# One table for the small weights, a later place for a split chunk's second value copies and for the zero block

## The chip, the cores and the metric

The kernel runs on one core of a Trainium2 chip. The metric is the time of one execution in device microseconds (us). Engines are named as the profile names them: PE is TensorE's matmuls and PEld its weight loads, DVE is VectorE, ACT is ScalarE, POOL is GpSimd, SP is SyncE, which here only issues transfers (DMAs).

## The reference

Three stages follow each other. Linear attention on q, k, v of shape (4, 8, 576, 64); an expert layer that sends each of the 2304 tokens to one of 8 experts (at most 576 tokens each); and a dense layer with a gate `h - tanh(h)`.

```
def phi(x):
    proj = np.einsum('bhsd,df->bhsf', x, w_phi)          # w_phi: 64 x 128
    proj = proj - np.max(np.abs(proj), axis=-1, keepdims=True)
    return np.concatenate([np.exp(proj), np.exp(-proj)], axis=-1)
q_p, k_p = (phi(q), phi(k))
kv = np.einsum('bhsf,bhsd->bhfd', k_p, v);  z = np.sum(k_p, axis=2)
out = einsum(q_p, kv) / (einsum(q_p, z) + 1e-06)
...
logits = x @ w_gate                                      # w_gate: 512 x 8
expert_idx = np.argmax(logits, axis=1)                   # then relu(x @ w1) @ w2 of that expert
...
h = x @ w_in;  out = (h - np.tanh(h)) @ w_out
```

## The kernel before

The 2304 tokens are 18 chunks of 128 rows. The attention is a loop over steps s = 0, 1, ... (line 761). Step s projects the keys of chunk s (`proj`, line 311, PE), subtracts the row maxima (`sub`, lines 319 and 322, DVE), takes both exponentials (`kexp`, lines 333 and 334, ACT), and sums keys times values of the chunk before into PSUM (`kv_step`, line 359, PE). From step 5 on (`LAG = 5`) the same step also projects the queries of chunk s - 5, transposes and exponentiates them (line 397), forms the numerator (`num`, line 458) and stores the rows (`xs`, line 536). Beside this a conversion works through the dense layer's weights, one piece a step: four transfers bring a piece (line 119, `raw`), and lines 93 (ACT), 98 to 106 (DVE, POOL), 282 (ACT) and 285 (POOL) turn it into two fp32r halves.

The expert logits are linear in v, so `vgate` (line 343, PE) multiplies each chunk's values by `w_gate` and ACT copies the result, and a column of ones, into the value tile beside the values (lines 347 and 350), before `kv_step` uses it. In steps 0 to 4 `vgate` stands ahead of the step's exponentials, from step 5 on behind them. Chunks 4 and 13 lie across two batches. They have two value tiles, one for each batch, with 64 rows each; `kv_step` uses the first and `kv_second` the second, after the first batch's sums are copied out (line 369).

Two small weights are needed at once: `wphi` (w_phi twice, one copy in each half of the partitions), for line 311, and `wgb` (w_gate laid out as blocks between zeros), for line 343. They come by four transfers on ACT's queue (lines 207 and 209); `wgb` is set to zero by DVE first. All other loads go out on SP's queue in the order of the program. Each transfer of the SP and ACT queues takes the next of eight semaphores in turn, so an issue waits until the transfer that had the same semaphore has landed; it also waits for its buffer. Keys, queries and transposed values have two buffers each, `raw` has two pieces, value tiles are three. The tile `d` between lines 322 and 333 has one buffer for the keys, and so has the result `kp` of lines 333 and 334 in most steps.

A block of zeros, `zs` (128 x 512 f32), is written to DRAM in step 7 (line 854). It is read much later, when the output is cleared (line 1179).

Nothing plans the order: each engine runs its instructions as the program issues them, and waits only on semaphores.

Of the kernel before, what the change touches and what calls it, by code (L numbers as in the profile page):

```python
# [8 lines left out]
F32 = mybir.dt.float32  # L9
# [7 lines left out]
P = 128  # L17
B, H, S, D = 4, 8, 576, 64
NT = B * S
DM = H * D  # L20
DF = 128
E = 8
FF = 1024
FF2 = 2048
NCH = NT // P
# [9 lines left out]
S2, T2 = -2.33084472, 2.44485132  # L35


def build(nc, tc, ctx, qT, kT, vT, v, w_phi, w_gate, w12, win, wout, out, cap):
    capn = min(cap, NT)
    G = max(1, -(-capn // UNIT))  # L40
    SL = G * UNIT
# [31 lines left out]
    sb = psp.tile([P, 512], F32, name="sb")  # L73
# [68 lines left out]
    def attention():  # L142
        st, stq = ExitStack(), ExitStack()
        LAG = 5
        ca = st.enter_context(tc.tile_pool(name="ca", bufs=1))
# [13 lines left out]
        HB = D + 1 + E  # L159
# [3 lines left out]
        GP = 2 * E  # L163
        PRE, CNT = 64, 512 - E

        wphi = ca.tile([P, DF], F32, name="wphi")
        wgb = ca.tile([P, 4, GP], F32, name="wgb")
        tri = ca.tile([P, P], BF16, name="tri")
        ones = ca.tile([P, P], BF16, name="ones")
        e16 = ca.tile([P, E], F32, name="e16")  # L170
# [4 lines left out]
        cum = ca.tile([P, E], BF16, name="cum")  # L175
        zero = ca.tile([P, P], F32, name="zero")

        nc.vector.memset(wgb, 0.0)
        nc.vector.memset(zero, 0.0)
        nc.vector.memset(ones, 1.0)  # L180
        nc.vector.memset(sq_b[:, 0:1], S1)
# [3 lines left out]
            out=tri, in_=ones, compare_op=ALU.is_gt, fill=0.0, base=0,  # L185
# [17 lines left out]
        nc.gpsimd.iota(tokv[:, :, 1], pattern=[[0, NCH]], base=0, channel_multiplier=1,  # L203
                       allow_small_or_imprecise_dtypes=True)

        for j in range(2):
            nc.scalar.dma_start(out=wphi[64 * j:64 * j + 64], in_=w_phi)
        for j in range(2):
            nc.scalar.dma_start(out=wgb[64 * j:64 * j + 64, :, j * E:(j + 1) * E],
                                in_=w_gate[:, 64 * j:64 * j + 64].rearrange("c p e -> p c e"))  # L210

        kin, qin, vtin = {}, {}, {}
        NV = 3
# [1 line left out]
        strad = {4: (0, 1), 13: (2, 3)}  # L215

        vuse, vslot, nv, done = {}, {}, 0, {}
# [12 lines left out]
        def ldk(c):  # L230
            t = ink.tile([P, DM], F32, tag="k", name="k")
            nc.sync.dma_start(out=t, in_=kT[c])
            kin[c] = t
# [44 lines left out]
        def cv_main(i):  # L278
            yield from cv_bits(raw.pop(i), cva.pop(i), cvm.pop(i))

        def cv_hi(i):
            nc.scalar.copy(pieces[i][1], cvw[i])
# [24 lines left out]
        def proj(kind, i, ps):  # L307
            src = (kin if kind == "k" else qin)[i]
            for hp in range(4):
                for g in range(2):  # L310
                    nc.tensor.matmul(ps[:, g, hp * DF:(hp + 1) * DF],  # L311
                                     src[64 * g:64 * g + 64, hp * P:(hp + 1) * P], wphi[64 * g:64 * g + 64],
                                     start=(hp == 0), stop=(hp == 3), skip_group_check=True)
            psk[kind, i] = ps.rearrange("p g (a b) -> p (g a) b", b=DF)
# [12 lines left out]
        def kexp(i):  # L327
            t = kd.pop(("k", i))
            if i in (1, 3):
                e = qp_p.tile([P, 2, H, P], F32, tag="qp", name="qp").rearrange("p s h f -> p h s f")  # L330
            else:
                e = kp_p.tile([P, H, 2, DF], F32, tag="kp", name="kp")
            nc.scalar.activation(out=e[:, :, 0, :], in_=t, func=AF.Exp)
            nc.scalar.activation(out=e[:, :, 1, :], in_=t, func=AF.Exp, scale=-1.0)
            kp[i] = e

        def vgate(c):
            vg = sb[:, 0:4 * GP].rearrange("p (a b) -> p a b", b=GP)
            ps = vg[:, :, 0:2 * E].rearrange("p a (b e) -> p a b e", e=E)
            for hp in range(4):  # L340
                for a in range(2):
                    o = hp * P + 64 * a
                    nc.tensor.matmul(vg[64 * a:64 * a + 64, hp, :], vtin[c][:, o:o + 64], wgb[:, hp],
                                     start=(hp == 0), stop=(hp == 3), skip_group_check=True)
            for a, t in enumerate(vuse[c]):
                lo, hi = (64 * a, 64 * a + 64) if c in strad else (0, P)
                nc.scalar.copy(t[lo:hi, :, D:D + 1], ones[lo:hi, 0:H].unsqueeze(2))
            for a, t in enumerate(vuse[c]):
                lo, hi = (64 * a, 64 * a + 64) if c in strad else (0, P)
                nc.scalar.copy(t[lo:hi, :, D + 1:HB].rearrange("p (a b) e -> p a b e", b=2), ps[lo:hi])  # L350

        def kv(i, vt, first, last):
            for g in range(2):
# [407 lines left out]
        for s in range(LAST + 1):  # L761
            i, j, jt = s, s - LAG, s - LAG - 1
            jn = jt if s < SD else jt - 1 if s > SD else -1
            kk, qq, tt = i < NCH, 0 <= j < NCH, 0 <= jt < NCH
            pc, pd = CV.get(s), CV.get(s - 1)
            since = {cs: s - (cs[-1] + LAG + 1) for cs in subs}
            if s == SK:
                stk.close()
                mo["alloc"]()
                qpools.append(stq.enter_context(tc.tile_pool(name="qp2", bufs=1)))  # L770
                mo["spare"](qpools[-1])
                mo["rows"](zero)
            if kk:
                proj("k", i, xb if i > LAG or i % 2 == 0 else yb)
            if s >= LAG:
                cv_load(s + 2 - LAG, 0, 1)
            if s + 2 < NCH:
                ldk(s + 2)
            if s >= LAG:
                cv_load(s + 2 - LAG, 2)  # L780
            if kk:
                if i < LAG:
                    vgate(i)
            if tt:
                trans(jt)
                qexp(jt, 0)
                qexp(jt, 1)
            if since[subs[-1]] == 3:
                prefix(early)
            if 0 <= i - 1 < NCH - 1:  # L790
                kv_step(i - 1)
            if kk:
                for _ in sub("k", i):
                    pass
            bits = iter(()) if pc is None else cv_main(pc)
            run(itertools.islice(bits, 2))
            if qq:
                proj("q", j, xb)
            if 0 <= j + 2 < NCH:
                ldq(j + 2)  # L800
            if s >= LAG:
                cv_load(s + 2 - LAG, 3)
            else:
                for k in ((), (0, 1), (2, 3), (4, 5), (6, 7))[s]:
                    cv_load(k // 4, k % 4)
            if i - 1 in strad:
                kv_second(i - 1)
            if i == NCH:
                kv_step(i - 1)
                first_ids()  # L810
            if pd is not None:
                cv_hi(pd)
                cv_lo(pd)
            if kk:
                kexp(i)
            wgen = iter(())
            if since[subs[-1]] == 3:
                wgen = itertools.chain(route2(early), table(early))
                run(itertools.islice(wgen, 5))
            if qq:  # L820
                for _ in sub("q", j):
                    pass
            smalls = []
            for cs in subs:
                d = since[cs]
                if d == 1:
                    rgen[cs] = route1(early, cs[0], cs[-1] + 1)
                if 1 <= d <= 3 and cs in rgen:
                    cut = (5,) if cs == subs[-1] else (2, 5)
                    smalls.append(itertools.islice(rgen[cs], *cut[d - 1:d]) if d <= len(cut) else rgen[cs])  # L830
            smalls.append(wgen)
            if s == NCH:
                smalls.append(fgen["t"])
            if s == SK:
                smalls.append(fgen["u"])
            weave([], smalls)
            flush()
            for _ in bits:
                pass
            if 0 <= jn < NCH:  # L840
                num(jn)
            if LAG <= i < NCH:
                vgate(i)
            if CV.get(s + 1) is not None:
                cv_mag(CV[s + 1])
            if s == SK:
                mo["first"]()
            if s + 2 < NCH:
                ldvt(s + 2)
            for c, a in vslot.get(s, []):  # L850
                if c > 1:
                    ldv(c, a)
            if s == 7:
                nc.sync.dma_start(out=zs.rearrange("t (a b) -> t a b", a=4),
                                  in_=zero.unsqueeze(1).to_broadcast([P, 4, P]))
            if 0 <= jn < NCH:
                xstore([jn])
            while rstore:
                rstore.pop()()
            if s >= SK:  # L860
                mo["drain"](s - SK)
            if s == SK + 3:
                rgen["a"] = route1(tailg, 0, NA)
                run(itertools.islice(rgen["a"], 5))
            if s == SK + 4:
                run(rgen["a"])
# [559 lines left out]
```

## Time and profile before

| what | us |
|---|---|
| median of three runs | 674.19 (674.09 to 676.39) |
| the profiled execution | 675.93 |
| its span, first to last instruction | 674.2 |
| PE busy | 642.6 (95%) |
| DVE busy | 522.3 (77%) |
| ACT busy | 411.9 (61%) |

The span is from the first to the last instruction; 1.7 us of the execution lie outside. The attention steps fill about the first 180 us. PE's share of busy time covers stages with different limits, and a matmul counts as busy for longer when the granted clock is low, so each stage is read by itself. In the windows the columns are busy time of each engine with its number of instructions, then the granted TensorE clock as a share of full speed (1.00 is 2.4 GHz, 0.50 is 1.2 GHz), the mean busy share of the 16 DMA engines, and GB/s. A row of the timeline gives start, busy time, engine, line, operation, tiles and count, and in brackets how long the engine was idle before it and what released it. A row marked SPq or ACTq is the issue of a transfer, not its landing.

### The profile page before, as it was taken

To read this page: it belongs to the slowest core of one execution; us is meant where nothing else is said; L and a number is where in the kernel's file an instruction comes from. 1 tells how busy PE (TensorE), PEld (TensorE's weight loads), DVE (VectorE), ACT (ScalarE), POOL (GpSimd) and SP (SyncE) were. 2 spreads that over 40 slices of the span, in tenths; PEclk is the share of its full clock that TensorE was granted. 3 is DMA by queue.
4 is the path that set the end of the run, shared out by engine and by line. 5 is a ranking of instruction groups with operands and counts; after the bars stand their busy time and mean duration, and the time that the engine had idled before them with its cause. 6 is when DMAs were issued, how large, how long until landed. Compare 5 with 4: busy or idle time off the path is not lost. (4 is left out here: it accounts for less than half of the span.)

```text
span 674.2 us, 17422 instructions
## 1 busy us (share of the span) xinstructions
PE 642.6 (95%) x7107; PEld 626.3 (93%) x7107; DVE 522.3 (77%) x773; ACT 411.9 (61%) x720; POOL 241.4 (36%) x182
## 2 busy tenths in 40 slices
PE   8799899998999999999999999999999999999993
PEld 7798888887999999999999999999999999999992
DVE  3789799997877879989876648888976547888982
ACT  3567887776744576677554536668645527658661
POOL 1255555554200234524530104633460102553361
PEclk7999899999999999999999999999999999999998
DMA  7969788725455634222225500101214530100221
GB/s 222 321 210 298 249 278 272 245 72 182 131 166 186 189 112 150 86 68 80 74 60 166 182 17 32 37 1 40 80 48 152 168 107 1 41 13 1 87 70 40
DMA packets 45481, 83.12 MB, mean 123 GB/s; under 512 B 7840, under 2 KB 8480, under 8 KB 45392
## 3 DMA queue, kind: packets, MB, share of 16 engines
q1 hardware_dynamic: 39664, 68.99, 32.4%
q0 software_dynamic: 2624, 8.13, 4.2%
q10 hardware_dynamic: 3104, 4.80, 2.1%
q8 instruction: 58, 0.95, 0.6%
q14 instruction: 31, 0.25, 0.1%
HBM read 73.31 MB, written 13.31 MB: 128 GB/s over the span
## 5 line engine op out<-in xcount | busy, mean ns | idle before, releaser
L1029 POOL TENSOR_SCALAR al<-ut 128x576 fp32r<-128x576 f32 (+1 forms) x51 | 84.1, 1649 | 152.2 <-ACT ut L1025 82.8
L924 DVE TENSOR_TENSOR w<-raw,w 128x512 fp32r<-128x512 f32 x102 | 71.1, 712 | 44.2 <-ACT w L919 43.6
L919 ACT CAST w<-raw 128x512 fp32r<-128x512 f32 x102 | 61.9, 620 | 60.2 <-DMA raw<-w 30.0
L937 PE MATMUL xb<-xh,w_in_h 128*128 128x288 f32 x264 | 79.5, 301 | 1.1 <-ACT ut L1025 1.1
L939 PE MATMUL xb<-xh,w_in_l 128*128 128x288 f32 x264 | 78.3, 297 | 0.0
L938 PE MATMUL xb<-xl,w_in_h 128*128 128x288 f32 x264 | 78.2, 296 | 0.0
L1076 POOL DMA_INDIRECT out<-row,ids x18 | 20.3, 1126 | 114.7 <-DVE row L1074 76.6
L1016 DVE TENSOR_TENSOR al<-y,ah 128x576 fp32r<-128x576 f32 (+1 forms) x51 | 40.4, 792 | 24.6 <-ACT ah L1015 24.6
L1024 ACT COPY hs<-xb 128x576 f32<-128x576 f32 (+1 forms) x36 | 21.6, 599 | 59.1 <-DVE th L1047 30.3
L319 DVE TENSOR_REDUCE m<-xb 128x8 f32<-128x1024 f32 x33 | 40.3, 1221 | 18.1 <-PE xb L311 17.9
L938 PE MATMUL kvb<-al,w_oa_h 128*128 128x288 f32 x180 | 53.4, 297 | 0.3 <-DVE al L1016 0.3
L939 PE MATMUL kvb<-ah,w_oa_l 128*128 128x288 f32 x180 | 53.3, 296 | 0.0
L937 PE MATMUL kvb<-ah,w_oa_h 128*128 128x288 f32 x180 | 53.2, 295 | 0.0
L1040 DVE SCALAR_TENSOR_TENSOR y<-y,ut 128x576 f32<-128x576 f32 (+1 forms) x51 | 41.3, 811 | 13.4 <-ACT y L1028 13.4
L937 PEld LDWEIGHTS xb<-xh,w_in_h 128*128 128x128 f32 x264 | 49.8, 189 | 1.3 <-ACT ut L1025 1.3
L1043 DVE SCALAR_TENSOR_TENSOR y<-y,y 128x576 f32<-128x576 f32 (+1 forms) x51 | 44.9, 879 | 7.4 <-ACT y L1030 5.6
L938 PEld LDWEIGHTS xb<-xl,w_in_h 128*128 128x128 f32 x264 | 49.7, 188 | 0.0
L939 PEld LDWEIGHTS xb<-xh,w_in_l 128*128 128x128 f32 x264 | 49.6, 188 | 0.0
L359 PE MATMUL kvb<-v,kp 128*64 128x74 f32 x1152 | 43.9, 237 | 4.0 <-issue 3.3
L359 PEld LDWEIGHTS kvb<-v,kp 128*64 128x64 f32 x1152 | 40.9, 144 | 6.8 <-issue 5.5
L1048 DVE COPY_PREDICATED y<-al,th 128x576 f32<-128x576 int32 (+1 forms) x51 | 42.8, 839 | 5.6 <-DVE th L1047 0.5
L1030 ACT ACTIVATE y<-ut,sq_b 128x576 f32<-128x576 f32 (+1 forms) x51 | 38.1, 748 | 13.3 <-DVE al L1016 11.2
(292 smaller groups left out, 2148.5 us busy)
## 6 DMA issues: line engine op xcount, KB each, us to landing
raw<-w SPq DMA_DIRECT2D x105, 256.0 KB
raw<-win SPq DMA_DIRECT2D x32, 256.0 KB
raw<-wout SPq DMA_DIRECT2D x20, 256.0 KB
v<-v SPq DMA_DIRECT2D x16, 296.0 KB
k<-kT SPq DMA_DIRECT2D x18, 256.0 KB
vt<-vT SPq DMA_DIRECT2D x18, 256.0 KB
q<-qT SPq DMA_DIRECT2D x18, 256.0 KB
xs<-x SPq DMA_DIRECT2D x18, 256.0 KB
```

The lines of the kernel that those rows point to most:

```text
L319: nc.vector.tensor_reduce(out=m, in_=ps, axis=AX.X, op=ALU.max, apply_absolute_value=True)
L359: nc.tensor.matmul(kvb[bank][64 * a:64 * a + 64, col * NKV:col * NKV + VS], kp[i][:, 4 * g + hp, s, 64 * a:64 * a + 64], vt[:, 2 * hp + g, :],
L919: nc.scalar.copy(d[:, 0], t)
L924: eng.tensor_tensor(out=d[:, 1], in0=t, in1=d[:, 0].bitcast(F32), op=ALU.subtract)
L937: nc.tensor.matmul(o, ah, bh, start=first, stop=False, skip_group_check=True)
L938: nc.tensor.matmul(o, ah, bl, start=False, stop=False, skip_group_check=True)
L939: nc.tensor.matmul(o, al, bh, start=False, stop=last, skip_group_check=True)
L1016: nc.vector.tensor_tensor(out=AL[a][:, i], in0=y2[:, i], in1=AH[a][:, i].bitcast(F32), op=ALU.subtract)
L1029: nc.gpsimd.tensor_scalar(out=AL[a][:, i], in0=ut[:, i], scalar1=C2, scalar2=None, op0=ALU.is_gt)
L1040: nc.vector.scalar_tensor_tensor(out=y1[:, i], in0=y1[:, i], scalar=T1, in1=ut[:, i], op0=ALU.add, op1=ALU.mult)
L1043: nc.vector.scalar_tensor_tensor(out=y2[:, i], in0=y2[:, i], scalar=T2, in1=y1[:, i], op0=ALU.add, op1=ALU.mult)
L1048: nc.vector.copy_predicated(y2[:, i], AL[a][:, i].bitcast(I32), th[:, i])
```

## The change

The host packs w_phi (twice) and the laid-out w_gate, zeros and all, into one table of 128 x 192 f32; one transfer brings it into one tile `small`, of which `wphi` and `wgb` are slices. The DVE memset of `wgb` goes. The value copies move into a function `vcopy(c, a)`. For chunk 4 the copies of the second value tile stand behind the step's exponentials; for chunk 13 they stay where they were, with the two pairs in another order. The first two pieces of `raw` are fetched on another schedule: two transfers in each of steps 0, 1, 2 and one in each of steps 3 and 4, instead of two in each of steps 1 to 4. The zero block goes out in step 18 instead of step 7.

```
-        for j in range(2):
-            nc.scalar.dma_start(out=wphi[64 * j:64 * j + 64], in_=w_phi)
-        for j in range(2):
-            nc.scalar.dma_start(out=wgb[64 * j:64 * j + 64, :, j * E:(j + 1) * E],
-                                in_=w_gate[:, 64 * j:64 * j + 64].rearrange("c p e -> p c e"))
+        nc.scalar.dma_start(out=small, in_=w_small)
...
-        nc.vector.memset(wgb, 0.0)
...
+        def vcopy(c, a):
+            vg = sb[:, 0:4 * GP].rearrange("p (a b) -> p a b", b=GP)
+            ps = vg[:, :, 0:2 * E].rearrange("p a (b e) -> p a b e", e=E)
+            t = vuse[c][a]
+            lo, hi = (64 * a, 64 * a + 64) if c in strad else (0, P)
+            nc.scalar.copy(t[lo:hi, :, D:D + 1], ones[lo:hi, 0:H].unsqueeze(2))
+            nc.scalar.copy(t[lo:hi, :, D + 1:HB].rearrange("p (a b) e -> p a b e", b=2), ps[lo:hi])
...
+            vcopy(c, 0)
+            if c >= LAG and c in strad:
+                vcopy(c, 1)
...
-                for k in ((), (0, 1), (2, 3), (4, 5), (6, 7))[s]:
+                for k in ((0, 1), (2, 3), (4, 5), (6,), (7,))[s]:
                     cv_load(k // 4, k % 4)
...
             if kk:
                 kexp(i)
+                if i < LAG and i in strad:
+                    vcopy(i, 1)
...
-            if s == 7:
+            if s == NCH:
                 nc.sync.dma_start(out=zs.rearrange("t (a b) -> t a b", a=4),
                                   in_=zero.unsqueeze(1).to_broadcast([P, 4, P]))
```

ACT at the start of the program, before: the four weight transfers, the table of the activation function, and the first value tile's column of ones and logits.

```order
L207 DMA wphi<-w_phi 64x128 x2
L209 DMA wgb<-w_gate 64x4x8 x2
L729 ACT_TABLE_LOAD
L729 ACTIVATE few<-few 128x8
L347 CAST v_156<-ones 128x8
L350 COPY v_156<-sb 128x8x8
```

The same place in the changed kernel:

```order
L205 DMA small<-w_small 128x192
L728 ACT_TABLE_LOAD
L728 ACTIVATE few<-few 128x8
L337 CAST v_151<-ones 128x8
L338 COPY v_151<-sb 128x8x8
```

Three issues are gone from ACT's queue, and the line numbers of the rest are lower by a few.

ACT around step 4, before. `v_157` and `v_158` are the first and the second value tile of chunk 4; `kp` is the exponentials, and the last row is the conversion of the next piece.

```order
L93 ACTIVATE a<-raw 128x1024
L347 CAST v_157<-ones 64x8
L347 CAST v_158<-ones 64x8
L350 COPY v_157<-sb 64x8x8
L350 COPY v_158<-sb 64x8x8
L333 ACTIVATE kp<-d 128x8x128
L334 ACTIVATE kp<-d 128x8x128
L93 ACTIVATE a<-raw 128x1024
```

The same place in the changed kernel, where the two tiles are `v_152` and `v_153`:

```order
L93 ACTIVATE a<-raw 128x1024
L337 CAST v_152<-ones 64x8
L338 COPY v_152<-sb 64x8x8
L328 ACTIVATE kp<-d 128x8x128
L329 ACTIVATE kp<-d 128x8x128
L337 CAST v_153<-ones 64x8
L338 COPY v_153<-sb 64x8x8
L93 ACTIVATE a<-raw 128x1024
```

The two copies into the second tile have moved from ahead of the exponentials to behind them, ahead of the conversion.

SP's queue from the end of step 0 to the middle of step 2, before (k: keys, vt: transposed values, v: value tile).

```order
L232 DMA k<-kT 128x512
L237 DMA vt<-vT 128x512
L246 DMA v_158<-v 128x592
L232 DMA k<-kT 128x512
L119 DMA raw<-win 128x512 x2
L237 DMA vt<-vT 128x512
L246 DMA v_156<-v 128x592
L232 DMA k<-kT 128x512
L119 DMA raw<-win 128x512 x2
L237 DMA vt<-vT 128x512
```

The same place in the changed kernel:

```order
L227 DMA k<-kT 128x512
L119 DMA raw<-win 128x512 x2
L232 DMA vt<-vT 128x512
L241 DMA v_153<-v 128x592
L227 DMA k<-kT 128x512
L119 DMA raw<-win 128x512 x2
L232 DMA vt<-vT 128x512
L241 DMA v_151<-v 128x592
L227 DMA k<-kT 128x512
L119 DMA raw<-win 128x512 x2
```

Two `raw` transfers have moved into step 0, behind the keys of chunk 2 and ahead of the transposed values and the value tile of that chunk. The zero block stands in SP's queue between two query loads of the last attention steps instead of between a value tile and a row store. On PE and POOL the sequence is the same in both kernels.

## Rows read from the trace of the kernel before

**Rows 1.** The page, busy time and share of each engine.

```profile
PE 642.6 (95%) x7107; PEld 626.3 (93%) x7107; DVE 522.3 (77%) x773; ACT 411.9 (61%) x720; POOL 241.4 (36%) x182
```

**Rows 2.** Windows: busy (x count) of PE, PEld, DVE, ACT, POOL; clock, DMA, GB/s.

```profile
0.00:10.00 10.00, 6.92 (x59) 5.56 (x61) 3.10 (x8) 2.78 (x5) 1.72 (x15) 0.86 0.67 203
10.00:20.00 10.00, 10.00 (x206) 9.37 (x204) 4.95 (x5) 4.99 (x10) 0.58 (x1) 0.79 0.83 253
20.00:30.00 10.00, 7.65 (x192) 7.02 (x190) 8.14 (x8) 4.77 (x10) 1.29 (x2) 1.00 0.99 316
30.00:40.00 10.00, 8.43 (x176) 7.98 (x176) 6.11 (x7) 6.67 (x10) 4.01 (x2) 0.83 0.61 212
140.00:160.00 20.00, 17.79 (x379) 16.36 (x379) 18.45 (x39) 13.72 (x22) 8.86 (x6) 1.00 0.27 74
```

**Rows 3.** One window of one microsecond, shortly ahead of step 6.

```profile
35.00:36.00 1.00, 1.00 (x24) 0.92 (x21) 0.00 (x0) 1.00 (x3) 0.00 (x0) 1.00 0.02 6
```

**Rows 4.** Timeline of steps 0 and 1.

```profile
0.81 1.24 ACTq L207 DMA_DIRECT2D wphi<-w_phi  x2
...
2.08 1.32 ACTq L209 DMA_DIRECT2D wgb<-w_gate  x2
...
4.22 0.48 PE L311 MATMUL xb<-wphi,k 64*128 64x128 f32 x2
...
5.42 1.16 PE L311 MATMUL xb<-wphi,k 64*128 64x128 f32 x14 [0.71 <-DMA wphi<-w_phi]
...
7.34 0.20 ACT L347 CAST v<-ones 128x8 f32<-128x8 bf16 x1 [2.39 <-DMA v<-v]
...
7.75 1.04 PE L343 MATMUL sb<-wgb,vt 128*64 128x16 f32 x16 [1.18 <-DMA wgb<-w_gate]
...
8.72 2.08 PE L311 MATMUL yb<-wphi,k 64*128 64x128 f32 x16
...
9.13 1.06 ACT L333 ACTIVATE kp<-d 128x1024 f32<-128x1024 f32 x1
...
11.60 3.45 PE L359 MATMUL kvb<-v,kp 128*64 128x74 f32 x64
```

**Rows 5.** Timeline of steps 4 and 5, up to the first row of step 6.

```profile
23.27 0.47 SPq L246 DMA_DIRECT2D v<-v  x1
...
25.45 1.23 DVE L322 TENSOR_TENSOR d<-xb,m 128x1024 f32<-128x1024 f32 x1
...
29.05 1.22 DVE L319 TENSOR_REDUCE m<-yb 128x8 f32<-128x1024 f32 x1
...
29.33 0.20 ACT L347 CAST v<-ones 64x8 f32<-64x8 bf16 x1 [3.63 <-DMA v<-v]
...
30.03 1.06 ACT L333 ACTIVATE kp<-d 128x1024 f32<-128x1024 f32 x1
...
32.06 1.23 DVE L322 TENSOR_TENSOR d<-yb,m 128x1024 f32<-128x1024 f32 x1 [1.79 <-ACT kp L334]
...
32.08 3.33 PE L359 MATMUL kvb<-v,kp 128*64 128x74 f32 x60 [0.39 <-ACT kp L334]
33.20 0.68 DVE L98 TENSOR_SCALAR m<-raw 128x1024 int32<-128x1024 int32 x1
...
36.43 2.27 PE L359 MATMUL kvb<-v,kp 128*64 128x74 f32 x64
...
38.76 1.06 ACT L333 ACTIVATE kp<-d 128x1024 f32<-128x1024 f32 x1 [1.94 <-PE kvb L359]
...
39.09 1.16 PE L311 MATMUL xb<-wphi,k 64*128 64x128 f32 x16
```

**Rows 6.** Timeline of steps 7 to 9.

```profile
58.19 0.60 SPq L854 DMA_DIRECT2D zs<-zero  x1
...
68.68 1.17 ACT L93 ACTIVATE a<-raw 128x1024 f32<-128x1024 f32 x1 [3.71 <-DMA raw<-win]
...
71.73 3.88 PE L458 MATMUL yb<-kvs,qp 128*64 128x74 f32 x64 [1.90 <-ACT qp L397]
```

More of the change, by code (lines that the diff above doesn't have):

```diff
@@ L35, with build @@
 S2, T2 = -2.33084472, 2.44485132
-def build(nc, tc, ctx, qT, kT, vT, v, w_phi, w_gate, w12, win, wout, out, cap):
+def build(nc, tc, ctx, qT, kT, vT, v, w_small, w12, win, wout, out, cap):
     capn = min(cap, NT)
@@ L164, in attention @@
         PRE, CNT = 64, 512 - E
-        wphi = ca.tile([P, DF], F32, name="wphi")
-        wgb = ca.tile([P, 4, GP], F32, name="wgb")
+        small = ca.tile([P, DF + 4 * GP], F32, name="small")
+        wphi, wgb = small[:, 0:DF], small[:, DF:].rearrange("p (c e) -> p c e", c=4)
         tri = ca.tile([P, P], BF16, name="tri")
@@ L335, in kexp @@
             kp[i] = e
+        def vcopy(c, a):
[5 more added lines that the diff above has]
+            nc.scalar.copy(t[lo:hi, :, D + 1:HB].rearrange("p (a b) e -> p a b e", b=2), ps[lo:hi])
         def vgate(c):
             vg = sb[:, 0:4 * GP].rearrange("p (a b) -> p a b", b=GP)
-            ps = vg[:, :, 0:2 * E].rearrange("p a (b e) -> p a b e", e=E)
             for hp in range(4):
@@ L344, in vgate @@
                                      start=(hp == 0), stop=(hp == 3), skip_group_check=True)
[L345 to L350, printed above, removed]
+            vcopy(c, 0)
+            if c >= LAG and c in strad:
+                vcopy(c, 1)
         def kv(i, vt, first, last):
@@ L1395, in rows_of_v, with small_weights @@
         return r.reshape(NCH, P, H * 74)
+    def small_weights(phi, gate):
+        r = np.zeros((2, D, 2 * D + 8 * E), np.float32)
+        r[:, :, 0:2 * D] = np.asarray(phi)
+        g = r[:, :, 2 * D:].reshape(2, D, 4, 2, E)
+        for a in range(2):
+            g[a, :, :, a] = np.asarray(gate).reshape(4, 2, D, E)[:, a].transpose(1, 0, 2)
+        r[:, :, 2 * D:] = g.reshape(2, D, 8 * E)
+        return r.reshape(2 * D, -1)
     def bits(a, kt):
@@ L1408 @@
         "v": rows_of_v(inputs["v"]),
-        "w_phi": np.ascontiguousarray(inputs["w_phi"]),
-        "w_gate": np.ascontiguousarray(inputs["moe_w_gate"]).reshape(4, P, E),
+        "w_small": small_weights(inputs["w_phi"], inputs["moe_w_gate"]),
         "w12": np.ascontiguousarray(np.concatenate([w1, w2], axis=-1)),
```

## The prediction

> **What bounds the kernel now.** I read the page first: over the whole span PE is busy for 95% [rows 1]. That is a mean over stages. The windows of the first 40 us show the stage that the change touches: there PE is busy for less, part of the time at 0.83 to 0.86 of its clock, and the DMA share goes from 0.67 to 0.99 and back to 0.61 [rows 2]. So neither PE nor the transfers are full all the time; something holds both up in turn. The timeline of the same stretch shows what. In step 0 it is the small weights. The first two matmuls run at 4.22, the other fourteen wait until 5.42 for the second piece of `wphi`, and the gate product waits 1.18 more for `wgb`, until 7.75. Then step 1's projection takes 2.08 and the first sum of keys and values 3.45 [rows 4], where the same work takes 1.16 and 2.27 at full clock [rows 5]. In step 4 it is a value tile. The subtraction is done at 26.68 (25.45 + 1.23), and ACT could take the exponentials then. But it stands at the copy into the second tile of chunk 4, whose load went out at 23.27, until 29.33, and takes them at 30.03 [rows 5]. By 35 the DMA engines are idle [rows 3]. After that the steps repeat, each released by the one before, and in step 8 a conversion waits 3.71 for its piece [rows 6]. Nothing in the stages behind is tied to a clock time, so what is won by the start of step 6 is a shift of all the rest, unless a later wait eats it.
>
> **Part A, one table.** Four issues become one, the DVE memset goes, and ACT is idle there anyway, so only the landing counts. The table is 98 KB, one piece of `wphi` 33 KB. The first piece, issued at 0.81, was there at 4.22, the second at 5.42. I take 4.4 for the table: 4.22 and the 65 KB that it has more, at the 316 GB/s of the full window [rows 2], 0.2. The projection then runs from 4.4 to 5.6 instead of ending at 6.58, 1.0 earlier. The gate product follows without its wait, and step 1's projection starts near 6.6 instead of 8.72. The first exponentials go from 9.13 to 8.1 (their value tile is there at 7.34) and end at 10.1. The sum behind them starts at 10.2 instead of 11.60 and ends at 12.5 at full clock or 13.7 at half clock, instead of 15.05. That is 2.6 or 1.4. PE again stands for some 2 us ahead of it, as it did ahead of the slow rows, so I take 1.4. With a table that lands at 5.42 only 0.4 is left.
>
> Below that there is one more case. The value tile, issued on SP's queue in the same first microseconds, landed at 7.34 [rows 4]. A table that comes in no earlier than that would start the first projection 1.9 later; the gate's wait would still go, and step 1's projection would start near 9.4 instead of 8.72, so A would be -0.7. The Trainium skill has a rule on this side, in DMA: Bandwidth & Descriptors, section Issuing engines are not separate DMA queues: whoever issues them, transfers run on the same 16 DMA engines and mix. By it the table shares them with 1.1 MB of SP's loads; by the row of 4.22 a small piece came through 3.1 us ahead of the last of these. The sum would be 3.8 by the late end and 5.9 by mine.
>
> Two `raw` transfers now go out in step 0, ahead of chunk 2's transposed values and value tile. They are 0.52 MB, 1.7 us at 316 GB/s. What hides them is the idle share of the first window (0.67 busy) and the slow steps 1 and 2. If that cover is gone, they cost up to 1.7. I take nothing.
>
> **Part B, the second copies.** Without the wait ACT takes the exponentials of step 4 from 26.7 to 28.7 (they take 2.0, 30.03 to 32.06). DVE is the next to be late: the three conversion operations and the reduction that stand behind the subtraction end at 30.27 (29.05 + 1.22), so the subtraction of step 5 moves from 32.06 only to 30.3, 1.8. PE starts the sum at 28.7, needs 2.27, and with the query projection (1.16) is at 32.1. DVE is busy with its subtraction until 31.5 and with two conversion operations of 0.7 until 32.9, and then reduces and subtracts the queries (1.23 each) until 35.4. Step 6's projection waited for just that at 39.09, so it is 3.7 earlier. If PE falls to half clock in this shorter pause, the sum takes 3.5 (3.33 for 60 of the 64) and the projection 1.2 to 2.1, and the gain is 3.2 to 2.3. PE's pause is about 1 us instead of 3.5, so I take 3.4.
>
> The copies now stand behind the exponentials, ahead of the next conversion and of the copying out of the sums. The load took 6.1 from its issue at 23.27 to 29.33; with one `raw` of 0.8 less ahead of it, it lands near 28.5, just when ACT comes to it at 28.7. Issue and exponentials move together by A. The copying out needs PE's sum, at 31.0, so 2.3 of delay cost little. Chunk 13's other order costs nothing: its copies wait for no transfer. If the tile held the exponentials' followers as long as before, B would be 0.
>
> **Part C, the zero block.** Its issue took 0.60 and it moved 0.26 MB, 0.8 at 316 GB/s, at 58.19. The conversion that waits 3.71 at 68.68 has its four transfers behind it on the same queue. So the wait shrinks by 0.8 to 1.4, unless the queue drains between, then by 0. PE's sum behind this wait ran 3.88 instead of some 2.3 [rows 6]; should a shorter wait spare that, another 1.6 comes, 3.0 in all. I take 1.1. In its new place it stands between query loads where the DMA share is 0.27 [rows 2], so it costs nothing, at most its 1.4.
>
> **The sum.** 1.4 + 3.4 + 1.1 = 5.9. The profiled execution took 675.93 (span 674.2), which would become 670.0. It lies 1.74 above the median of the runs, 674.19, so the median becomes 668.3.
>
> **Rivals.** First, the transfers are the bound and the gain is given back. Up to 40 us they moved 10 us x (203 + 253 + 316 + 212) GB/s = 9.84 MB. At 316 from 2 us on, that is done at 33.1, ahead of the 34.3 at which I have step 6 start (39.09 - 4.8). But if the first 20 us stay at their mean of 228, 4.56 MB are moved by 20 and the rest takes until 36.7. Then step 6 gains only 2.4, and C nothing since the queue is never empty: 671.8. For it speaks the share of 0.99 in the third window; against it, the idle engines at 35 and that the table lets loads go out earlier. The Trainium skill, DMA: Bandwidth & Descriptors, section Specifications, gives about 358 GB/s as a core's share of the memory; an estimate with that figure is 29.5 for the 9.84 MB, and no window of 10 us here reaches it.
>
> Second, the change does only part of what it says: the table lands at 5.42 and PE stays at half clock in both places. Then A is 0.4, B 2.3 and C 0: 671.5. For it speaks that the second piece did land at 5.42 and that PE still pauses; against it, that it was issued 0.6 after the first.
>
> Third, slower: the two `raw` transfers of step 0 make chunk 2's loads late, and PE waits for transfers in steps 2 to 4. The price is the 1.7 and the half clock that follows a pause: 1.2 for a sum (3.45 against 2.27) and 0.9 for a projection (2.08 against 1.16), 2.1 a step, 6.3 for three. Those 8.0 against B and C (4.5) give 677.7. It decides from the point where the transposed values of chunk 2 land later than its projection ends, near 14. Against it: they were loaded in SP's order after 8.8 before, and the matmuls of steps 1 and 4 show no wait for a load [rows 4, 5].
>
> **How the numbers follow.** My forecast has 0.73, the transfers 0.10, the half effect 0.11, the slower case 0.06. A measurement of this kernel can tell 0.5%, 3.4 us, from no change, so the borders are 670.8 and 677.6. The forecast lies below 670.8 in nearly all of its span: its best end is 2.6 + 3.7 + 3.0 = 9.3, or 664.9; the late table, to which I give 0.08 of the 0.73, gives 674.19 - 3.8 = 670.4. The two middle rivals are within 0.5%. So faster 0.73, the same 0.21, slower 0.06. The range goes from 664.0, a little past the best end, to 672.5, past both middle rivals, since 0.27 of the chance lies beyond 670.8.
>
> **What would show it.** In the changed profile: the first projection runs its 16 matmuls in one go before 5; no gate wait; the exponentials of step 4 start within 0.3 of the subtraction's end; the copies into the second tile come behind them; step 6's projection starts at 33 to 36; the wait in step 8 is under 3. I am wrong if step 6 starts after 37, if the projection starts after 5.4, or if step 6 is early but the attention ends as late as before, since then waits for `raw` took the gain back.

## The result and the profile after

The changed kernel took 669.08 us (median of 16 runs, 665.93 to 673.46), the kernel before 674.86 in the same comparison (16 runs, 671.17 to 679.13). The medians are 5.8 apart, the means 6.3. The ratio, which goes with the means, is 0.9907 (95% interval 0.9885 to 0.9930): 6.3 us faster. A second comparison (`again`, below) gave 0.9904, interval 0.9877 to 0.9932. The profiled execution after has a span of 668.3.

The page's row of busy times after:

```profile
PE 637.6 (95%) x7107; PEld 620.9 (93%) x7107; DVE 524.1 (78%) x772; ACT 411.4 (62%) x720; POOL 240.5 (36%) x182
```

The windows of the first 40 us after, with the columns of [rows 2]:

```profile
0.00:10.00 10.00, 7.35 (x83) 5.57 (x83) 4.15 (x8) 3.36 (x6) 1.69 (x15) 1.00 0.81 260
10.00:20.00 10.00, 8.74 (x220) 8.25 (x222) 4.99 (x5) 5.30 (x11) 0.58 (x1) 1.00 0.95 307
20.00:30.00 10.00, 9.57 (x228) 8.77 (x226) 8.37 (x8) 6.79 (x10) 2.94 (x2) 1.00 0.96 295
30.00:40.00 10.00, 9.05 (x206) 8.23 (x206) 9.84 (x10) 9.06 (x14) 5.30 (x3) 1.00 0.84 270
```

The clock is 1.00 throughout, against 0.86, 0.79, 1.00 and 0.83 [rows 2], and the DMA share has no hole.

The timeline of steps 0 and 1 after, which answers to [rows 4]:

```profile
0.81 0.41 ACTq L205 DMA_DIRECT2D small<-w_small  x1
...
4.43 1.45 PE L306 MATMUL xb<-small,k 64*128 64x128 f32 x16
...
5.81 0.65 PE L345 MATMUL sb<-small,vt 128*64 128x16 f32 x16
...
6.39 1.16 PE L306 MATMUL yb<-small,k 64*128 64x128 f32 x16
6.59 0.20 ACT L337 CAST v<-ones 128x8 f32<-128x8 bf16 x1 [3.84 <-DMA v<-v]
...
10.50 2.15 PE L358 MATMUL kvb<-v,kp 128*64 128x74 f32 x60 [0.60 <-ACT kp L329]
...
12.58 1.16 PE L306 MATMUL xb<-small,k 64*128 64x128 f32 x16
```

The reader is to see that the first projection runs its 16 matmuls in one piece at 4.43, that the gate product waits for nothing, that step 1's projection comes 2.3 earlier, and that the first sum takes 2.15 for 60 matmuls where it took 3.45 for 64.

The four transfers before cost one more wait, which the rows ahead of the prediction do not show. In the list of waits of SP's queue before (total, times, longest), the issue of the transposed values of chunk 1 stands until a piece of `wphi` has landed; it is the ninth transfer, and the semaphores go round by eight:

```profile
SPq L237 <- DMA wphi<-w_phi: 1.2, 1, 1.2
```

That issue is at 3.99 before and at 2.66 after, where the list has no such wait.

The timeline of steps 4 and 5 after, which answers to [rows 5]:

```profile
21.28 0.47 SPq L241 DMA_DIRECT2D v<-v  x1
...
23.76 1.23 DVE L317 TENSOR_TENSOR d<-xb,m 128x1024 f32<-128x1024 f32 x1
...
25.02 1.06 ACT L328 ACTIVATE kp<-d 128x1024 f32<-128x1024 f32 x1 [0.58 <-DVE d L317]
...
27.05 0.20 ACT L337 CAST v<-ones 64x8 f32<-64x8 bf16 x1
...
27.07 2.15 PE L358 MATMUL kvb<-v,kp 128*64 128x74 f32 x60 [0.34 <-ACT kp L329]
...
27.36 1.22 DVE L314 TENSOR_REDUCE m<-yb 128x8 f32<-128x1024 f32 x1
...
28.69 1.23 DVE L317 TENSOR_TENSOR d<-yb,m 128x1024 f32<-128x1024 f32 x1
...
28.91 1.17 ACT L93 ACTIVATE a<-raw 128x1024 f32<-128x1024 f32 x1 [1.43 <-DMA raw<-win]
...
33.04 1.06 ACT L328 ACTIVATE kp<-d 128x1024 f32<-128x1024 f32 x1 [0.73 <-PE kvb L358]
...
33.74 1.16 PE L306 MATMUL xb<-small,k 64*128 64x128 f32 x16 [0.32 <-DVE d L317]
```

The first `L328` stands right behind the subtraction (23.76 + 1.23 = 24.99). The copy at 27.05 comes behind the exponentials and waits for nothing. The last row is the first of step 6, 5.4 earlier than before.

To see where the gain came and went, the table gives the start of a step's key projection (the first of 16 matmuls), read from the timelines. Later steps have their own waits.

| kernel | step 2 | 5 | 6 | 8 | 10 | 13 | 17 | span |
|---|---|---|---|---|---|---|---|---|
| before | 14.98 | 26.67 | 39.09 | 56.27 | 75.99 | 101.89 | 138.39 | 674.2 |
| after | 12.58 | 25.30 | 33.74 | 50.51 | 67.19 | 94.16 | 131.84 | 668.3 |
| gain | 2.4 | 1.4 | 5.4 | 5.8 | 8.8 | 7.7 | 6.6 | 5.9 |

So 1.4 are won by step 5, 4.0 between 5 and 6, 3.0 between 8 and 10, and 2.2 of it are lost again by 17.

At step 2 the gain was 2.4, and 1.0 of it is gone by step 3. Before, the sum of keys and values in step 2 ran in one piece:

```profile
16.56 2.25 PE L359 MATMUL kvb<-v,qp 128*64 128x74 f32 x64
```

After, it stops behind 45 of its 64 matmuls, for nothing that the profile shows ("issue"), and ends 3.28 after its start:

```profile
14.16 1.67 PE L358 MATMUL kvb<-v,qp 128*64 128x74 f32 x45
...
16.58 0.86 PE L358 MATMUL kvb<-v,qp 128*64 128x74 f32 x19 [0.76 <-issue]
```

The same stop is in `again` (0.54) and `u_copy` (1.03). What PE stands for there is open.

Three rows after tell of the last two stretches: the conversion in step 8 waits 2.22 instead of 3.71 [rows 6], the sum behind it takes 2.31 instead of 3.88, and a conversion in step 12 waits 3.89 (the steps of conversions are counted as in the prediction, by the step that issues them). The timeline and the issue of the zero block after:

```profile
61.43 1.22 ACT L93 ACTIVATE a<-raw 128x1024 f32<-128x1024 f32 x1 [2.22 <-DMA raw<-win]
...
64.52 2.31 PE L457 MATMUL yb<-kvs,qp 128*64 128x74 f32 x64 [0.45 <-ACT qp L396]
...
98.26 1.16 ACT L93 ACTIVATE a<-raw 128x1024 f32<-128x1024 f32 x1 [3.89 <-DMA raw<-wout]
...
143.84 0.60 SPq L855 DMA_DIRECT2D zs<-zero  x1
```

### The profile page after: what moved, and what is told of

It is laid out like the page before. It is cut to its first block, busy times and chain, and to the rows that moved or that the text cites. A ratio compares the mean times of both kernels' runs of the same rounds, so it can differ in the third digit from the quotient of the medians.

```text
span 668.3 us, 17411 instructions
## 1 busy us (share of the span) xinstructions
PE 637.6 (95%) x7107; PEld 620.9 (93%) x7107; DVE 524.1 (78%) x772; ACT 411.4 (62%) x720; POOL 240.5 (36%) x182
## 5 line engine op out<-in xcount | busy, mean ns | idle before, releaser
L938 PE MATMUL yb<-xh,w 128*128 128x288 f32 x144 | 43.8, 304 | 0.7 <-DVE al L985 0.7
L938 PE MATMUL kvb<-ah,w 128*128 128x288 f32 x144 | 42.6, 296 | 1.8 <-ACT ah L984 1.0
```

The costliest lines, as they stand in the source:

```text
L938: nc.tensor.matmul(o, ah, bh, start=first, stop=False, skip_group_check=True)
```

## The experiments

Each ratio is of the kernel's runs to runs of the kernel before on the same chip. The measured points of all of them (the columns of steps 5, 6 and 17 are the starts of their key projections, "8 to 10" is the time between two such starts):

| kernel | ratio (95%) | step 5 | step 6 | 8 to 10 | step 17 | span |
|---|---|---|---|---|---|---|
| u_copy | 0.9946 (0.9920 to 0.9972) | 26.02 | 34.55 | 17.2 | 131.87 | 667.5 |
| u_zs | 0.9915 (0.9883 to 0.9948) | 27.57 | 36.35 | 17.5 | 133.78 | 666.5 |
| u_raw | 0.9926 (0.9901 to 0.9951) | 26.12 | 35.03 | 16.8 | 132.53 | 664.3 |
| u_table | 0.9925 (0.9898 to 0.9952) | 27.93 | 36.70 | 16.7 | 132.78 | 666.4 |
| o_copy | 0.9958 (0.9931 to 0.9986) | 26.92 | 36.63 | 17.2 | 133.81 | 668.5 |
| o_table | 0.9952 (0.9925 to 0.9978) | 25.39 | 37.23 | 16.9 | 134.44 | 666.5 |
| o_raw | 0.9996 (0.9969 to 1.0023) | 27.87 | 39.90 | 18.3 | 137.59 | 675.1 |
| o_zs | 1.0002 (0.9974 to 1.0030) | 26.99 | 39.48 | 17.0 | 138.03 | 671.8 |
| again | 0.9904 (0.9877 to 0.9932) | 25.48 | 33.84 | 16.3 | 131.14 | 664.2 |
| two | 0.9914 (0.9883 to 0.9945) | 26.04 | 36.11 | 20.2 | 135.11 | 669.1 |
| b_part3 | 0.9861 (0.9835 to 0.9888) | 25.58 | 34.34 | 16.2 | 129.93 | 662.9 |
| o_part3 | 0.9975 (0.9950 to 1.0001) | 26.91 | 39.24 | 17.6 | 137.12 | 671.9 |

From step 17 to the end of the span lie 531.8 (u_raw) to 537.5 (o_raw) in these profiles, in no order that goes with the edits. So a span of one execution says little to 3 us, and the starts of the early steps more; the ratios speak for the time.

**u_copy**: the change with the copies back ahead of the exponentials.

```
-            vcopy(c, 0)
-            if c >= LAG and c in strad:
-                vcopy(c, 1)
+            for a in range(len(vuse[c])):
+                vcopy(c, a)
...
-                if i < LAG and i in strad:
-                    vcopy(i, 1)
```

> The change with chunk 4's second copies back ahead of the exponentials. If the parts add up (my theory): step 5 starts near 25.3 as in the change, the exponentials of step 4 wait for the tile again, step 6 starts near 37 to 38 instead of 33.7, and the time is 3 to 4 us above the change, ratio to before 0.996 to 0.998. If instead the other schedule of the raw transfers frees the tile (it lands earlier), the wait is under 1 us, step 6 starts before 35 and the ratio stays near 0.991.

The timeline of its step 4, the two columns of ones and the first exponentials:

```profile
24.86 0.19 ACT L337 CAST v<-ones 64x8 f32<-64x8 bf16 x1
...
26.20 0.20 ACT L337 CAST v<-ones 64x8 f32<-64x8 bf16 x1 [1.05 <-DMA v<-v]
...
26.67 1.06 ACT L328 ACTIVATE kp<-d 128x1024 f32<-128x1024 f32 x1
```

The wait for the second tile is 1.05, not 3.63, and step 6 starts at 34.55. In the profile the rival holds: with the table and the other `raw` schedule the tile lands nearly in time by itself. The ratio lies between the two expectations, 0.9946; those of u_zs, u_raw and u_table, measured beside it, are 0.002 to 0.003 lower, with intervals that overlap. Whether other executions wait longer than the profiled one stays open.

**u_zs**: the change with the zero block back in step 7.

```
-            if s == NCH:
+            if s == 7:
                 nc.sync.dma_start(out=zs.rearrange("t (a b) -> t a b", a=4),
```

> The change with the zero block back in step 7. My theory: step 8 starts near 50.5 as in the change, step 10 is 1 to 3 us later than the change's 67.2, and the time is 1 to 3 us above the change, ratio to before 0.992 to 0.995. If the gain of the change between steps 8 and 10 was only another pattern of waits for the conversion's pieces, step 10 and the time stay within 1 us of the change (ratio 0.990 to 0.992).

Up to step 7 this is the program of the change, and yet steps 2 and 5 start at 15.03 and 27.57. Its timeline of steps 0 to 2:

```profile
4.43 2.08 PE L306 MATMUL xb<-small,k 64*128 64x128 f32 x16
...
10.19 0.51 PE L358 MATMUL kvb<-v,kp 128*64 128x74 f32 x4 [1.38 <-ACT kp L328]
...
11.13 3.97 PE L358 MATMUL kvb<-v,kp 128*64 128x74 f32 x60 [0.43 <-ACT kp L329]
...
15.03 2.01 PE L306 MATMUL xb<-small,k 64*128 64x128 f32 x16
```

The first sum takes 3.97 for 60 matmuls, and the projection of step 2 takes 2.01: half clock, after nearly the same pauses of PE as in the profile after (1.38 and 0.43 here, 1.43 and 0.60 there). The windows from 12 to 16 us have a granted clock of 0.50 here,

```profile
12.00:16.00 4.00, 4.00 (x60) 3.85 (x58) 0.34 (x1) 2.10 (x3) 0.00 (x0) 0.50 0.76 282
```

and of 1.00 in the profile after:

```profile
12.00:16.00 4.00, 3.83 (x98) 3.54 (x94) 2.11 (x2) 2.06 (x4) 0.00 (x0) 1.00 0.98 327
```

The 2.08 of the first projection is another matter: the clock was 1.00 there, and what slowed it is not shown. From step 8 to 10 the kernel takes 17.5, 0.8 more than the change; step 10 is 2.8 later, as my theory allowed, but 2.0 of that stood at step 8. The ratio, 0.9915, is where the second expectation had it and cannot be told from the change's.

**u_raw**: the change with the old `raw` schedule.

```
-                for k in ((0, 1), (2, 3), (4, 5), (6,), (7,))[s]:
+                for k in ((), (0, 1), (2, 3), (4, 5), (6, 7))[s]:
```

> The change with the raw transfers on their old schedule. My theory, which gave this part nothing: the start of step 6 within 1 us of the change's 33.7, ratio 0.990 to 0.993. If the two transfers in step 0 hurt steps 2 and 3 (step 3 of the change starts at 17.4, 4.8 after step 2), step 3 starts near 16.4 and step 6 near 32.7, ratio 0.989. If the schedule is what lets the second value tile land in time, the copies hold ACT, and with it the conversion and the copying out of the sums, by 1 us or more, and step 6 starts at 35 or later.

Step 6 is at 35.03, 1.3 later than in the change: just past the 1 us that my theory allowed, and where the third expectation had it; the ratio is 0.9926, as my theory had it. But the copies do not hold ACT, which was that expectation's reason: the first into the second tile runs at 28.18 without a wait. Behind them the conversion waits 1.98 for its own piece:

```profile
30.59 1.16 ACT L93 ACTIVATE a<-raw 128x1024 f32<-128x1024 f32 x1 [1.98 <-DMA raw<-win]
```

**u_table**: the change with four transfers for the small weights and the memset.

```
-        nc.scalar.dma_start(out=small, in_=w_small)
+        for j in range(2):
+            nc.scalar.dma_start(out=wphi[64 * j:64 * j + 64], in_=w_phi)
+        for j in range(2):
+            nc.scalar.dma_start(out=wgb[64 * j:64 * j + 64, :, j * E:(j + 1) * E],
+                                in_=w_gate[:, 64 * j:64 * j + 64].rearrange("c p e -> p c e"))
```

> The change with the small weights by four transfers again. My theory: the first projection ends near 6.6 again, step 2 starts near 15 and step 5 near 26.7, step 6 near 35.1, and the time is 1 to 2 us above the change, ratio 0.992 to 0.994. If the early gain is eaten by the transfers before step 6, step 6 starts within 0.5 of 33.7 and the ratio is 0.991.

Step 5 starts at 27.93, 1.2 later than expected and later than before. The early gain is lost and not eaten: step 6 is at 36.70. It seems that the `raw` transfers of step 0 cost about 1 when the small weights come by four transfers; o_raw, below, is the only other profile that has both. The ratio, 0.9925, is as expected and cannot be told from the change's.

**o_copy**: the kernel before with only the place of the copies changed (the diff of u_copy, turned round).

> The kernel before with only the second copies of chunk 4 behind the exponentials. My theory: step 5 starts near 26.7 as before, the exponentials of step 4 start right behind their subtraction, step 6 starts 3.4 to 3.7 earlier than 39.1, the time falls by 3 to 4 us, ratio 0.994 to 0.996. If the wait in the profile of before was a chance of that one execution, the gain of the copies alone is under 1.5 us, ratio 0.998 or more.

The timeline of its step 4, the first exponentials and the next conversion:

```profile
26.95 1.06 ACT L333 ACTIVATE kp<-d 128x1024 f32<-128x1024 f32 x1 [0.90 <-DVE d L322]
...
32.21 1.15 ACT L93 ACTIVATE a<-raw 128x1024 f32<-128x1024 f32 x1 [2.37 <-DMA vt<-vT]
```

The exponentials no longer wait for the tile. Step 6 starts 2.5 earlier, where 3.4 to 3.7 were expected, and the ratio is 0.9958: 2.8 us, at the low side of what my theory gave. The wait was no chance of one execution. Behind the copies the conversion now stands 2.37, which the profile puts down to a load; whether that took the missing 0.9 is not shown.

**o_table**: the kernel before with only the table (the diff of u_table, turned round).

> The kernel before with only the one table. Theory of the parts: steps 2 to 5 start 1.4 to 2.4 earlier than before if PE keeps its clock, and 0 to 0.5 earlier if it drops to half (step 5 at 25.3 or at 26.5), the wait of ACT for the second tile stays near 3.6 since load and exponentials move together, ratio 0.996 to 0.999. If the earlier loads are what takes the wait away (as the change with the copies put back suggests, where it was 1.05), the wait is under 1.5, step 6 starts before 36, ratio 0.993 to 0.995.

The timeline of its step 4, the column of ones of the second tile, and the first row of step 6:

```profile
27.49 0.20 ACT L337 CAST v<-ones 64x8 f32<-64x8 bf16 x1 [3.85 <-DMA v<-v]
...
37.23 1.16 PE L306 MATMUL xb<-small,k 64*128 64x128 f32 x16
```

Step 5 starts 1.3 earlier, and the wait is 3.85: load and exponentials have moved together, as expected. The ratio is lower than expected, 0.9952; 3.2 us, of which the steps up to 6 show 1.9.

**o_raw**: the kernel before with only the other `raw` schedule (the diff of u_raw, turned round).

> The kernel before with only the other schedule of the raw transfers. If it is one transfer fewer ahead of the tile that takes the wait away, ACT's wait in step 4 falls from 3.6 to about 1 and step 6 starts near 36.5. If the transfers in step 0 only stand in the way of the loads beside the four small ones (the change without the table started step 5 at 27.9), step 5 starts 1 later than 26.7 and step 6 at 37.5 to 39; ratio 0.997 to 1.001.

The column of ones of the second tile in step 4:

```profile
29.73 0.20 ACT L347 CAST v<-ones 64x8 f32<-64x8 bf16 x1 [2.84 <-DMA v<-v]
```

Step 5 starts 1.2 later, and the wait in step 4 is 2.84. So one transfer fewer ahead of the tile takes 0.8 of the wait and no more, and the loss before it takes that back; the ratio is 0.9996.

**o_zs**: the kernel before with only the zero block moved (the diff of u_zs, turned round).

> The kernel before with only the zero block moved to step 18. My theory: up to step 8 as before (56.3), the wait in step 8 falls from 3.7 to about 2.5, step 10 starts 1 to 3 earlier than 76.0, ratio 0.996 to 0.998. If that wait was one of the waits for pieces that come and go from run to run, steps 8 to 10 take 17 to 18 us with or without the block, and the ratio is 0.998 to 1.001.

The conversion of step 8:

```profile
68.13 1.20 ACT L93 ACTIVATE a<-raw 128x1024 f32<-128x1024 f32 x1 [2.50 <-issue]
```

It stands 2.50 instead of 3.71, as expected, though the profile names no transfer that ended it. Steps 8 to 10 take 17.0 instead of 19.7, and yet step 17 starts at 138.03, where it was 138.39, and the ratio is 1.0002. What is won by step 10 is lost again by 17.

**again**: the changed kernel once more.

> The changed kernel itself once more, for a second profile of the same program beside the others of this call. If the clock in the first 16 us is the same in every execution, steps 2 and 5 start at 12.6 and 25.3 again; if it differs between executions, as the change with the zero block put back suggests (same program up to step 7, steps 2 and 5 at 15.0 and 27.6), step 2 may lie anywhere from 12.6 to 15.1. The waits for raw pieces in steps 6 to 14 (7.0 in four in the first profile, one of 3.9) should sum to 5 to 9 again, not in the same steps. Ratio 0.989 to 0.993.

The clock was whole again, step 5 is at 25.48. The waits before the conversion (its line 93) come in the same steps as in the first profile this time, one of 3.05 in step 12 among them, which the profile puts down to a row store. What I expected of their pattern is wrong. Those put down to `raw` sum to 5.9 from 30 to 140 us and the ratio is 0.9904, both as expected.

**two**: the kernel before with the table and the place of the copies; the change with the edits of u_raw and u_zs.

> The kernel before with the table and the place of the second copies, the raw schedule and the zero block as before. If these two parts are the whole gain and add (single ratios 0.9952 and 0.9958), the ratio is 0.990 to 0.993, the same as the change. If the raw schedule or the zero block adds to them in company, the ratio is 0.993 to 0.996.

The ratio is 0.9914: the two parts are the gain, as the first expectation had it, though the interval reaches into the second. The timeline of its step 8, where the conversion waits again with the block in step 7 (the profile names the row store as the last to land):

```profile
65.90 1.16 ACT L93 ACTIVATE a<-raw 128x1024 f32<-128x1024 f32 x1 [4.24 <-DMA xs<-x]
```

**b_part3**: the changed kernel with the fourth `raw` transfer ahead of the query load.

```
-                cv_load(s + 2 - LAG, 2)
+                cv_load(s + 2 - LAG, 2, 3)
...
-            if s >= LAG:
-                cv_load(s + 2 - LAG, 3)
-            else:
+            if s < LAG:
```

> The changed kernel with the fourth raw transfer of a piece ahead of the step's query load instead of behind it, so that it goes out 1 to 3 us earlier in steps 5 to 15. If the remaining waits of the conversion for its piece (about 7 to 10 in all) hang on that last transfer's place, they fall by 1 to 3 each, to under 4 in all, and the time falls by 2 to 5 us below the change (ratio to before 0.984 to 0.988). If the transfers' bandwidth is the bound there, the last transfer lands no earlier, or the query load now lands late, and the ratio stays at 0.989 to 0.993 or rises.

The list of waits of ACT's line 93 from 30 to 140 us (total, times, longest), first of the change:

```profile
ACT a L93 <- DMA raw<-win: 6.4, 4, 2.2
...
ACT a L93 <- issue: 4.0, 3, 1.9
ACT a L93 <- DMA raw<-wout: 3.9, 1, 3.9
```

and of this kernel:

```profile
ACT a L93 <- DMA raw<-win: 2.6, 4, 1.1
ACT a L93 <- DMA raw<-wout: 2.3, 2, 1.6
...
ACT a L93 <- issue: 1.8, 1, 1.8
```

From 14.3 to 6.7; in `again`, the other profile of the change, they sum to 14.3 as well. The time is 664.44 (663.58 to 665.86) against 666.93 (665.88 to 669.53) of the change measured beside it, ratio to before 0.9861. The waits hung on the place of that transfer, though they did not fall under the 4 expected. This version is faster than both kernels.

**o_part3**: the same edit alone, on the kernel before.

> The kernel before, zero block in step 7 and all, with only the fourth raw transfer ahead of the step's query load. If the wait of 3.7 in step 8 hung on that transfer's late place rather than on the zero block, it falls under 1.5, steps 8 to 10 take under 18 us (19.7 before), and the time falls by 2 to 4 us, ratio 0.994 to 0.997. If the zero block is what fills the queue there, the wait stays over 2.5, steps 8 to 10 take 19 or more, and the ratio is 0.997 to 1.001. Step 5 and step 6 start as before (26.7 and 39.1) by both.

The timeline of its steps 7 and 8, one conversion each:

```profile
59.23 1.17 ACT L93 ACTIVATE a<-raw 128x1024 f32<-128x1024 f32 x1 [3.22 <-POOL a L106]
...
66.70 1.18 ACT L93 ACTIVATE a<-raw 128x1024 f32<-128x1024 f32 x1 [0.82 <-DMA raw<-win]
```

The wait for the piece in step 8 is 0.82 with the zero block still in step 7, and steps 8 to 10 take 17.6. So in this profile the 3.71 of before hung on the late place of the transfer, more than on the block. But the conversion of step 7 now stands 3.22 behind POOL, where it stood 1.00 before. The ratio is 0.9975 and the interval ends at 1.0001: just outside the first expectation and inside the second, so the time does not decide between them.

## Why the prediction was right, point by point

The forecast was 668.3 and 5.9 us of gain; measured were 669.08 and, by the ratios, 6.3 and (in `again`) 6.5. That it fits so closely is partly luck: C alone gave nothing, A and B gave more than they were counted for, and the errors cancel. One reading in the prediction is off, without effect on the sum: the clock of the first windows goes down to 0.79, and PE is busy throughout in that one [rows 2].

**What bounded the early steps.** Right. Small weights and the second tile held the stage in turn, and most of what was won there reached the end.

**Part A, 1.4.** Met at step 5 (1.4 in the change, 1.3 alone), but by luck. The table landed by 4.43 where 4.4 was assumed; the late landing at 7.34 did not come, although the table shared the DMA engines with the first value tile, whose copy ran at 6.59. The prediction chose half clock and so 1.4. In the profile after the clock was full and step 2 gained 2.4, near the 2.6 worked out for that case; the stop in the sum of step 2 then took 1.0 back. Alone it went likewise: 2.1 at step 2, and PE stops 0.58 in the projection of step 4. The choice of the clock was the wrong question, since it differs between executions: `after`, `again`, u_zs and b_part3 are one program up to step 4, and their step 5 starts at 25.30, 25.48, 27.57 and 25.58, from 1.4 earlier to 0.9 later than before. Nor does only the landing count, as the prediction had it: the table also ends the 1.2 for which SP's queue stood; what that is worth, no run separates. The ratio of the table alone is larger than 1.4, 3.2 with an interval of 1.5 to 5.1; where the rest comes from in the steps behind is not shown.

**The `raw` transfers of step 0, "I take nothing".** Not contradicted beside the table. Without it they seem to cost: step 5 at 27.87 and 27.93 in two profiles, against 26.67 to 26.99 in the four with neither. For the wait in step 4 the prediction counted 0.8 for one `raw` fewer ahead of the tile, and alone the schedule took just that (3.63 to 2.84). What it had not is that together with the table the wait falls to 1.05 with the copies in their old place, while alone the table leaves 3.85; each is one profile. The third rival, slower by PE's waits for chunk 2, did not come: up to 40 us no wait of PE for a transfer stands in the profile after.

**Part B, 3.4.** Right in mechanism, somewhat large in size: alone 2.5 at step 6 and 2.8 in time, with an interval of 0.9 to 4.6. DVE's chain is the next to be late, as worked out: its reduction ends at 28.58 (27.36 + 1.22), and the subtraction of step 5 runs at 28.69. In the change the stretch from step 5 to 6 is 4.0 shorter, and in u_copy, with the copies in their old place, 3.9. So in these profiles the table and the schedule together take away nearly the same wait as the copies; the parts overlap, which the sum had not allowed for. Single profiles are rough here: u_raw and `two`, one program up to step 7, take 8.9 and 10.1 for this stretch.

**Part C, 1.1.** This is the step that failed, by its size. The wait shrank by 1.5 and the slow sum was spared, so that 3.0 were won from step 8 to 10, the upper bound. But it is not shown that they are the block's work: o_copy and o_table, with the block in step 7, take 17.2 and 16.9 there, `two` 20.2. And 2.2 were lost again by step 17, and alone the move has the ratio 1.0002 (0.9974 to 1.0030). Steps 8 to 17 take 79.9 to 81.3 in the six profiles of its kind without `b_part3` (after, again, u_copy, u_raw, u_table, o_zs) and 80.3 to 82.2 in the six with the block in step 7 (before, u_zs, o_copy, o_table, o_raw, two): means 80.7 and 81.3, so 0.6, within the spread. I had written that a later wait may eat the gain, and did not apply it to the one part that lies among such waits. The sum came out because A and B together gave more than their 4.8: 5.4 at step 6, and 6.0 by their single ratios (3.2 and 2.8; `two` has 5.8).

**The rival of the transfers.** Not before step 6: the DMA share rose to 0.81, 0.95 and 0.96, and step 6 started at 33.7, close to the 34.3 worked out. The windows of four microseconds of the kernel before show what the transfers can do:

```profile
20.00:24.00 4.00, 3.82 (x96) 3.46 (x94) 2.40 (x2) 2.44 (x5) 0.58 (x1) 1.00 1.00 306
24.00:28.00 4.00, 3.84 (x98) 3.56 (x96) 3.74 (x5) 1.70 (x3) 0.00 (x0) 1.00 0.97 295
28.00:32.00 4.00, 0.51 (x4) 0.32 (x4) 2.27 (x2) 2.60 (x6) 2.35 (x1) 0.90 1.05 386
32.00:36.00 4.00, 3.92 (x70) 3.84 (x72) 2.43 (x3) 2.63 (x6) 0.00 (x0) 0.68 0.54 199
```

The 386 GB/s lie above the 358 that the Trainium skill, DMA: Bandwidth & Descriptors, section Specifications, gives as a core's share of the memory; here the measurement decides, over four microseconds at least, and 29.5, the estimate with that figure, is no lower bound. Behind step 6 the rival holds in part: not by bandwidth but by the place of one transfer in the queue, as b_part3 shows.

## What to carry to other kernels

Where an engine works in order, a copy that waits for a load belongs behind the work that does not need it. A transfer that ends a wait should stand in its queue ahead of one that has steps to spare, as the fourth `raw` transfer does in b_part3 (14.3 to 6.7 of waits). What is won ahead of a stretch that has its own waits for loads must be followed to the end of that stretch before it is counted: the 2.7 that o_zs won between steps 8 and 10 were nothing at the end.

## What was not expected of the hardware

One program had full clock in one execution and half clock in another in the same stretch: from 11.1 to 15.0 us the first sum of u_zs ran 3.97 for 60 matmuls, where the change ran 2.15 from 10.5, after pauses of nearly the same length; the granted clock was 0.50 and 1.00. Step 5 starts 2.3 later there (27.57 against 25.30), which is more than part A itself, so a gain of that size can't be read from one profile's early steps. And in step 2 three profiles at full clock (`after`, `again`, u_copy) lost 0.8 to 1.3 again, where PE stopped for nothing that they show.
